# Own orders of a pair of steps for 0 to 6 products, both value bursts in its middle, and row maxima taken 22 steps ahead

## The chip, the cores and the metric

The kernel runs on one core of one Trainium2 chip. The metric is device time in microseconds (us) of one launch; lower is better. Three runs of the kernel before gave 1702.52, 1699.56 and 1701.65 us, so the median is 1701.65 us.

## The reference

```python
def _A_ref(x, wqkv, wo):                     # x (1, 2048, 512), H = 32 heads of Dh = 16
    qkv = (x @ wqkv).reshape(B, S, 3, H, Dh) ...
    scores = jnp.einsum("bhqd,bhkd->bhqk", q, k) * Dh ** -0.5
    p = softmax(scores, axis=-1)
    o = jnp.einsum("bhqk,bhkd->bhqd", p, v)
    return o.reshape(B, S, D) @ wo
def _B_ref(x, w1, b1, w2, b2):               # w1 (2048, 1792), w2 (1792, 2048)
    h = _layernorm(x)
    u = _gelu(jnp.einsum("bsd,sf->bdf", h, w1) + b1)
    return (jnp.einsum("bdf,fs->bds", u, w2) + b2).transpose
xn = _layernorm(x)
return x + _A_ref(xn, wqkv, wo) * _silu(_B_ref(xn, w1, b1, w2, b2))
```

Everything is float32, without a mask: full softmax attention over 2048 tokens with 32 narrow heads, and beside it a two-layer network that mixes tokens.

## The kernel before, in words

Large products are made in three parts from operands split into an upper and a lower half (`three`). The attention is walked in **steps**: one step is one block of 128 keys, for one span of 1024 queries and one pair of heads. There are 512 steps of scores (`NT`) and 512 steps of maxima (`NU`). Softmax needs each query's maximum first, so every score is computed twice:

- `max_of` (L390, L394) makes a 128x512 piece of scores with queries on the partitions, in one of three PSUM banks `mx`; VectorE (DVE) reduces it to one maximum a query.
- `max_rows` (L400 on) is called once in 16 steps. It reduces the collected maxima with a minus sign (L409), turns them by four 32x32 transposes (L406), splits them on GpSimd (POOL; L417, L79), and writes them by four DMAs as two extra rows of the query tile `big` (L83). It returns its work as three pieces, which the loop calls one at a time through `piece()`.
- `score` (L767, L772) makes the transposed piece with keys on the partitions and 50 rows of contraction, the maxima among them, in one of three PSUM banks `sc`. ScalarE (ACT) takes the exponential into a tile `prob`.
- `values` (L783) multiplies the four `prob` tiles of a step with the value block: eight matmuls of 128x32, four side by side. This is called a **burst** here. All 16 key blocks of a span accumulate in the one bank `av`; `put_away` (L522) then copies it out on ACT.

The maxima run `LEAD` = 20 steps ahead of the scores. The token mixer, and after it the output projection, are cut into single **products** (L921 in the main loop, L896 before and after it), which a generator hands out and `take` fetches. A **block** of products accumulates in the one bank `dn`: 48 products for each of the first 14 blocks, then 42 for each of 16, then 9 each for the first 11 blocks of the output projection. At a block's end ACT and POOL work on the result (`gelu`, `silu`, L506 and L507, or `part`), and `take` stops.

The main loop goes over s = 0, 2, 4, ...; two steps make a **pair**. A pair holds 8 maxima, 8 scores, 2 bursts, and n products. All engine queues are strictly in the order in which this loop emits. A product is split into two matmuls on rows 0-63 and 64-127 of the array (`halves`), the maxima and scores of head 0 lie on the lower half and of head 1 on the upper, and the two halves work at the same time. Two strings in `ORDERS`, one for each half, say what is emitted place by place: `D` a product's half, `m` a maximum, `s` a score. One place of the two strings is called a **slot** here. The number behind the strings is the slot ahead of which the first burst stands:

```python
6: ("DDDDDDsmsmsmsm", "msmsmsmsDDDDDD", 7),
```

The second burst stands at the end of the pair. `wanted` spreads the mixer's products up to step 442; what comes out is 6 products in most pairs, what is left (2 for the usual blocks) in the pair that ends a block, and 4 in the pair that begins one. For 5 products the order for 6 is used, with an empty place.

Ahead of the main loop, for s under `LEAD`, maxima alone are made, in groups of three pieces for each head with 11 whole products behind each group (`EARLY`). After step 512 a tail makes the last scores and bursts, with up to 12 whole products behind a burst.

Of the kernel before, what the change touches and what calls it, by code (L numbers as in the profile page):

```python
# [21 lines left out]
def tile_attention_token_mixer(ctx, tc, x, wqkv, wo, w1, b1, w2, b2, out):  # L22
# [7 lines left out]
    NB = S // P  # L30
# [3 lines left out]
    QH = S // 1024  # L34
    SPP = QH * NB
    NT = NP * SPP
    LEAD = 20
    N_BEFORE = 3
    scale = DH ** -0.5

# [113 lines left out]
    with (  # L154
# [214 lines left out]
    def after(n, f):  # L369

        later.append(f if n == 1 else lambda: after(n - 1, f))

    def run_later():
        now, later[:] = list(later), []
        for f in now:
            f()

# [18 lines left out]
    def max_rows(u):  # L396

        p, r = divmod(u // 2, NB)
        span = r // 8
        neg = negs[u // 16 % 2]  # L400
        f = sm.tile([32, P], F32, name="f", bufs=1)


        def turned(*blocks):
            for c in blocks:
                nc.vector.transpose(f[:, 32 * c : 32 * c + 32], neg[32 * c : 32 * c + 32, :])  # L406

        def one():
            nc.vector.tensor_reduce(  # L409
                neg[:, :16].rearrange("p (a b) -> p a b", a=2), mxp.pop(u // 16), axis=AX.X, op=OP.max, negate=True,  # L410
            )
            turned(0)

        def three_():
            turned(3)
            m = sm.tile([16, 2, P], F32R, name="m", bufs=1)
            nc.gpsimd.tensor_copy(m[:, 0, :], f[:16, :])  # L417
            sub(nc.gpsimd, m[:, 1, :], f[:16, :], m[:, 0, :])
            for a in range(2):
                for t in range(2):  # L420
                    row = 64 * a + 48 + t
                    move(
                        qs[p][row : row + 1, span * 1024 : (span + 1) * 1024],
                        m[8 * a : 8 * a + 8, t, :], nc.gpsimd,
                    )

        return one, lambda: turned(1, 2), three_

# [90 lines left out]
    def put_away(p, span, av):  # L519

        ev = el.tile([P, 512], F32, name="ev")
        nc.scalar.copy(ev, av)  # L522
        if p == NP - 1:
            own(span, ev)
            return
        g, i = divmod(p, 4)
        if i == 0:
            dens[span] = sm.tile([P, 64], F32, name="d")
        rows = ev.rearrange("(j r) q -> r j q", r=32)
        for a in range(2):  # L530
# [243 lines left out]
    def values(t):  # L774
        p, r = divmod(t, SPP)
        span, kb = divmod(r, NB)
        if kb == 0:
            state["av"] = ps_av.tile([P, 512], F32, name="av")
        av = state["av"]
        for a in range(2):  # L780
            for c in range(2):
                j = 2 * a + c
                nc.tensor.matmul(  # L783
                    av[32 * j : 32 * j + 32, :],
                    vps[p][:, kb, 16 * a : 16 * a + 32], prob.pop((t, a, c)),
                    start=kb == 0, stop=kb == NB - 1,
                )
        if kb == NB - 1:
            later.append(lambda: put_away(p, span, av))

    def rest():

# [65 lines left out]
    done = 0  # L858
    n_fill = NF * 3 * NB + NB * 3 * NF
    total = NT + LEAD  # L860
    T_MIX = NU - 70
    FIRST = 12
    EARLY = 11
    begun = []

    ended = [False]

    def take(n, each):
# [21 lines left out]
    def whole(x, then):  # L890
# [9 lines left out]


    ORDERS = {
        0: ("smsmsmsm", "msmsmsms", 3),
        2: ("smsmDDsmsm", "msmsmsmsDD", 3),
        4: ("sDDDDmsmsmsm", "msmsmsmDDDDs", 6),
        6: ("DDDDDDsmsmsmsm", "msmsmsmsDDDDDD", 7),
    }

    def halves(lead, n):

# [14 lines left out]
        take(n, each)  # L925
        return *parts, then

    def wanted(s):

        share = min(1.0, (s + 1 - LEAD) / (T_MIX - LEAD))  # L930
        if not begun:
            begun.append(done)
        start = begun[0]
        return start + share * (n_fill - start) + (6 if done == n_fill else 0) if share < 1 else done + 6

    def items(s, a):

# [16 lines left out]
    def piece():  # L954
        if pieces:
            pieces.pop(0)()
            return True
        return False

    lead = 0  # L960
    for s in range(0, total + 1, 2):
        t = s - LEAD
        now[0] = s
        run_later()
        if done >= n_fill // 2 + 3 * NF:
            divisions()
        if s >= NU - 12 and unkept:
            load_second()
        heads = [items(s, a) for a in range(2)]
        if s < NU and t >= 0:  # L970
            steady[0] = True
            late = ended[0]
            n = max(0, min(6, round((wanted(s + 1) - done) / 2) * 2))
            one, two, then = halves(lead, min(n, 4) if late else n)
            made = [dict(D=part, m=heads[a][0], s=heads[a][1]) for part, a in ((one, lead), (two, 1 - lead))]
            first, second, middle = ORDERS[(len(one) + 1) // 2 * 2]
            if one:
                lead = 1 - lead
            for i, kinds in enumerate(zip(first, second)):
                if i == middle:  # L980
                    now[0] = s + 1
                    piece()
                    if 0 <= t - 2 < NT:
                        values(t - 2)
                    run_later()
                for of, kind in zip(made, kinds):
                    if of[kind]:
                        of[kind].pop(0)()
                if "D" in kinds and not two:
                    for f in then:  # L990
                        f()
                    then = []
            for f in then:
                f()
        elif s < NU:

            for i in range(4):
                first_maxima.append((s + i // 2, i % 2))
                if len(first_maxima) == 3 or i == 3 and (s % 16 == 14 or s + 2 == LEAD):
                    for u, half in first_maxima:  # L1000
                        max_of(u, half, 0)
                        max_of(u, half, 1, ps_sc, "sc")
                    first_maxima.clear()
                    take(EARLY, whole)
                if i == 1:
                    now[0] = s + 1
                    run_later()
        else:
            made = [heads[a][1] for a in range(2)]
            n = len(made[0])  # L1010
            for i in range(n):
                made[1][i]()
                made[0][i]()
                if i == n - 2:
                    if not piece() and asides:
                        asides.pop(0)()
                    values(t - 2)
                    take(3 * ND, whole)
                    now[0] = s + 1
                    run_later()  # L1020
            if 0 <= t - 1 < NT and (t - 1, 0, 0) in prob:
                if n:
                    if not piece() and asides and s < total - 2:
                        asides.pop(0)()
                    values(t - 1)
                    if s == total - 2:
                        load_gates(NB // 2, NB - 2)
                    take(3 * ND, whole)
            if s == total - 6:
                split_last_w()  # L1030
        if s < NU and s % 16 == 14:
            pieces.extend(max_rows(s + 1))
        while piece() and t < 0:
            pass
        for v in (t - 2, t - 1):
            if 0 <= v < NT and (v, 0, 0) in prob:
# [16 lines left out]
    left = []  # L1053
    for k in range(4):
        chunk(ps, of, slice(k * P, (k + 1) * P))
    while open_ or later:
        run_later()
        take(3, lambda x, f: left.append(f) if f else whole(x, f))
    for f in left:
# [42 lines left out]
```

## Time and profile before

| | |
|---|---|
| median of three runs | 1701.65 us |
| profiled execution | 1699.51 us |
| its span, first to last instruction | 1697.7 us |
| mean granted TensorE clock | 0.997 |
| TensorE matmul (PE) / weight load (PEld) | 1662.0 us / 842.7 us |
| VectorE / ScalarE / GpSimd | 1425.0 / 1188.0 / 566.5 us |

Between the profiled execution and its span lie 1.8 us. The matmuls of the two halves overlap, and so do those of a burst, so the busy time of PE says only that some matmul was under way. In rows of the timeline the columns are start, duration, engine, line, operation, output and input, count, and in brackets the idle time ahead with what ended it.

### The profile page before, as it was taken

What the parts mean: (1) busy time and instruction counts of PE and PEld (TensorE: products, weight loads), DVE (VectorE), ACT (ScalarE), POOL (GpSimd) and SP (SyncE); (2) the same over time, 40 slices, a digit from 0 to 9 for tenths busy, and PEclk for the clock granted to TensorE, in tenths of its full rate; (3) what the DMA queues carried; (4) which work ended last, traced back from release to release, by engine and by line L of the source; (5) the groups of instructions that cost most, each with busy time, mean ns of one, the idle gap of its engine ahead of it and who ended that gap; (6) DMA issues with size and microseconds to landing.
All of it is one profiled execution on the core that took longest, in us unless ns stands there. A gap on an engine that the chain in (4) does not pass through costs nothing.

```text
span 1697.7 us, 30716 instructions
## 1 busy us (share of the span) xinstructions
PE 1662.0 (98%) x11693; PEld 842.7 (50%) x11693; DVE 1425.0 (84%) x2476; ACT 1188.0 (70%) x2292; POOL 566.5 (33%) x671
## 2 busy tenths in 40 slices
PE   7999999999999999989999999999999999999997
PEld 6887644444444444444444444444444444444443
DVE  6655998888888888878888888888889988889845
ACT  3332277777777777767777777777777777787764
POOL 3223843234342344323322322222222222372411
PEclk9999999999999999999999999999999999999999
DMA  6568612415150513553241514141412223273345
GB/s 211 186 238 190 131 35 57 73 45 85 45 80 26 92 46 54 148 128 91 60 82 53 92 35 76 35 83 35 66 48 43 52 50 68 82 147 102 116 139 197
DMA packets 151311, 153.72 MB, mean 91 GB/s; under 512 B 51500, under 2 KB 109868, under 8 KB 148092
## 3 DMA queue, kind: packets, MB, share of 16 engines
q1 hardware_dynamic: 146748, 151.02, 37.1%
q8 instruction: 92, 1.51, 0.4%
q0 software_dynamic: 4416, 0.75, 0.3%
q14 instruction: 55, 0.45, 0.1%
HBM read 100.81 MB, written 49.79 MB: 89 GB/s over the span
## 4 chain that ended last, share of the span: by engine, by line
PE 90%; DVE 5%; DMA 2%; ACT 1%; POOL 1%; issue 1%; SPq 0%; DVEq 0%; POOLq 0%
PE av L783 27%; PE dn L921 26%; PE mx L390 13%; PE sc L767 11%; DVE mxp L394 4%; PE dn L896 3%; PE mx L303 2%; PE sc L303 2%; PE av L896 1%; ACT prob L772 1%; PE dn L303 1%; PE av L303 1%; DMA big<-m 1%; PE mx L767 0%; PE sc L86 0%
## 5 line engine op out<-in xcount | busy, mean ns | idle before, releaser
L394 DVE TENSOR_REDUCE mxp<-mx 128x1 f32<-128x512 f32 x2008 | 1248.1, 681 | 164.8 <-PE mx L390 85.1
L772 ACT ACTIVATE prob<-sc 128x512 f32<-128x512 f32 x2008 | 1041.8, 604 | 330.4 <-PE sc L767 269.2
L390 PE MATMUL mx<-big 48*128 48x512 f32 x2008 | 827.7, 428 | 2.6 <-DVE mxp L394 0.8
L767 PE MATMUL sc<-big 50*128 50x512 f32 x2008 | 769.2, 427 | 8.2 <-DMA big<-m 6.7
L921 PE MATMUL dn<-hu,wh 64*128 64x512 f32 x1570 | 573.2, 405 | 0.0
L783 PE MATMUL av<-prob,vp 128*32 128x512 f32 x4096 | 546.0, 605 | 0.0
L390 PEld LDWEIGHTS mx<-big 48*128 48x128 f32 x2008 | 364.0, 186 | 222.3 <-DVE mxp L394 208.1
L767 PEld LDWEIGHTS sc<-big 50*128 50x128 f32 x2008 | 354.5, 185 | 195.2 <-ACT prob L772 170.6
L921 PEld LDWEIGHTS dn<-hu,wh 64*128 64x128 f32 x1570 | 288.7, 185 | 171.8 <-issue 144.9
L921 PE MATMUL dn<-hu,wl 64*128 64x512 f32 x786 | 315.7, 402 | 0.9 <-POOL wl L79 0.9
L148 POOL CAST wh<-raw 128x512 fp32r<-128x512 f32 x108 | 62.9, 583 | 319.3 <-PE dn L921 315.1
L79 POOL TENSOR_TENSOR wl<-raw,wh 128x512 fp32r<-128x512 f32 x124 | 150.4, 1216 | 38.0 <-ACT wh L150 22.7
L783 PEld LDWEIGHTS av<-prob,vp 128*32 128x32 f32 x4096 | 80.9, 108 | 154.9 <-issue 146.5
L921 PEld LDWEIGHTS dn<-hu,wl 64*128 64x128 f32 x786 | 145.6, 185 | 9.4 <-POOL wl L79 1.3
L417 POOL CAST m<-f 16x128 fp32r<-16x128 f32 x32 | 9.0, 280 | 281.2 <-DVE f L406 281.2
L474 POOL TENSOR_TENSOR sq<-u 128x512 f32<-128x512 f32 x14 | 14.6, 1040 | 200.3 <-ACT u L473 200.3
L83 POOL DMA_DIRECT2D big<-m x128 | 66.2, 524 | 0.0
L921 PE MATMUL dn<-wh,hu 64*128 64x512 f32 x132 | 45.7, 399 | 0.0
L79 POOL TENSOR_TENSOR hu<-hx,hu 128x512 fp32r<-128x512 f32 x16 | 20.4, 1290 | 57.1 <-ACT hu L246 57.1
L772 ACT ACTIVATE prob<-mx 128x512 f32<-128x512 f32 x40 | 24.7, 617 | 17.6 <-PE sc L767 9.5
L303 PE MATMUL mx<-xt,big 128*128 128x512 f32 x144 | 35.3, 393 | 0.0
L303 PE MATMUL sc<-xt,big 128*128 128x512 f32 x144 | 34.6, 389 | 0.0
(200 smaller groups left out, 1088.7 us busy)
## 6 DMA issues: line engine op xcount, KB each, us to landing
raw<-in_B_w_dram SPq DMA_DIRECT2D x104, 256.0 KB
big<-k_d SPq DMA_DIRECT2D x96, 128.0 KB
big<-q_d SPq DMA_DIRECT2D x96, 128.0 KB
q_d<-sg SPq DMA_DIRECT2D x16, 512.0 KB
k_d<-sg SPq DMA_DIRECT2D x16, 512.0 KB
num_d<-ev SPq DMA_DIRECT2D x30, 256.0 KB
u_d<-uo SPq DMA_DIRECT2D x14, 512.0 KB
hu<-u_d SPq DMA_DIRECT2D x14, 512.0 KB
```

What stands on the lines that cost most here:

```text
L79: eng.tensor_tensor(out=o, in0=a, in1=b.bitcast(F32), op=OP.subtract)
L83: queue.dma_start(dst.bitcast(F32), src.bitcast(F32))
L148: nc.gpsimd.tensor_copy(whs[n][:, :m, :], raws[n][:, :m, :])
L303: nc.tensor.matmul(ps, w[part][:, kd, m], xt[kd][:, z, :], start=w is wh and z == 0 and kd == 0, stop=w is wl and kd == ND - 1,)
L390: nc.tensor.matmul(ps, q[o : o + 48, r * P : (r + 1) * P], k[o : o + 48, c * 512 : (c + 1) * 512], start=True, stop=True,)
L394: nc.vector.tensor_reduce(mxp[u // 16][:, a, r % 8, c : c + 1], ps, axis=AX.X, op=OP.max)
L474: nc.gpsimd.tensor_tensor(out=sq, in0=u, in1=u, op=OP.mult)
L767: nc.tensor.matmul(ps, ks[p][o : o + 50, kb * P : (kb + 1) * P], qs[p][o : o + 50, at : at + 512], start=True, stop=True,)
L772: nc.scalar.activation(e, ps, AF.Exp, scale=scale)
L783: nc.tensor.matmul(av[32 * j : 32 * j + 32, :], vps[p][:, kb, 16 * a : 16 * a + 32], prob.pop((t, a, c)), start=kb == 0, stop=kb == NB - 1,)
L896: nc.tensor.matmul(ps, w(slice(0, P)), m(slice(0, P)), start=first, stop=last)
L921: made.append(lambda r=r, start=first and a == lead, stop=last and a != lead: nc.tensor.matmul(ps, w(r), m(r), start=start, stop=stop,))
```

## The change

- **Orders.** `ORDERS` has an entry for 0, 2, 3, 4, 5 and 6 products, and each names two slots: both bursts now stand inside the pair. `ENDS` has orders for a pair of 4 or 5 products that ends a block, `BEGINS` two for a pair of 4 that begins one; `order` chooses.
- **Counts.** `count` replaces `wanted`: a block is cut into 6 products a pair, except 4 in the pair that begins it and 4 and 4 in its last two (4 and 5 for blocks of nine).
- **Putting away.** The copy of a finished span goes to `soon`: two slots behind the second burst, or at the next call of `run_later`.
- **Maxima.** `LEAD` is 22. `max_rows` returns four pieces (the reduction, one transpose, two transposes, the last with the split and the DMAs), and one is called ahead of each of the two bursts; none at the pair's end any more.
- **Loading.** `load_second` starts at step 502 instead of 500.

```diff
-    LEAD = 20
+    LEAD = 22
...
-        return one, lambda: turned(1, 2), three_
+        return largest, lambda: turned(0), lambda: turned(1, 2), last
...
-            later.append(lambda: put_away(p, span, av))
+            soon.append(lambda: put_away(p, span, av))
...
     ORDERS = {
-        0: ("smsmsmsm", "msmsmsms", 3),
-        2: ("smsmDDsmsm", "msmsmsmsDD", 3),
-        4: ("sDDDDmsmsmsm", "msmsmsmDDDDs", 6),
-        6: ("DDDDDDsmsmsmsm", "msmsmsmsDDDDDD", 7),
+        0: ("ssmmmssm", "msmssmms", 3, 8),
+        2: ("mmsmDDsssm", "ssmsmsmmDD", 3, 10),
+        3: ("DDDsssmmsmm", "ssmmmmssDDD", 4, 7),
+        4: ("DDDDsmsmmssm", "smsmmsmsDDDD", 4, 7),
+        5: ("DDDDDmmsmsmss", "mmsmsssmDDDDD", 5, 8),
+        6: ("DDDDDDsmmsmsms", "msmssmmsDDDDDD", 4, 8),
     }
+    ENDS = {4: ("DDDDmsmssmms", "smsmsmDDDDsm", 4, 10), 5: ("DDDDDssssmmmm", "smsmsmmDDDDDs", 6, 12)}
+    BEGINS = [
+        {4: ("smDDDDsmsmms", "msmsmsmsDDDD", 1, 7)},
+        {4: ("DDDDmssmsmsm", "mmsssmsmDDDD", 5, 8)},
+    ]
+    def order(n, t, late, ends):
+        of = BEGINS[done > n_fill or t % NB == 2] if late else ENDS if ends else ORDERS
+        n = min(x for x in ORDERS if x >= n)
+        return of.get(n, ORDERS[n])
...
+    sizes = [3 * NB] * NF + [3 * NF] * NB + [3 * (ND - 1)] * PARTS
+    def count(late):
+        left = -done
+        for n in sizes:
+            left += n
+            if left > 0:
+                break
+        return 4 if late or left in (7, 8) else 5 if left == 9 else max(0, min(6, left))
...
-            for i, kinds in enumerate(zip(first, second)):
-                if i == middle:
-                    now[0] = s + 1
+            for i, kinds in enumerate((*zip(first, second), "")):
+                if i in places:
                     piece()
-                    if 0 <= t - 2 < NT:
-                        values(t - 2)
-                    run_later()
+                    v = t - 2 + places.index(i)
+                    if v >= 0:
+                        values(v)
+                    if v == t - 2:
+                        now[0] = s + 1
+                        run_later()
+                if i == places[1] + 2:
+                    while soon:
+                        soon.pop()()
...
-        while piece() and t < 0:
+        while t < 0 and piece():
```

More of the change, by code (lines that the diff above doesn't have):

```diff
@@ L371, in after @@
         later.append(f if n == 1 else lambda: after(n - 1, f))
+    soon = []
     def run_later():
-        now, later[:] = list(later), []
+        now, later[:] = soon + later, []
+        soon.clear()
         for f in now:
@@ L406, in turned, with largest @@
                 nc.vector.transpose(f[:, 32 * c : 32 * c + 32], neg[32 * c : 32 * c + 32, :])
-        def one():
+        def largest():
             nc.vector.tensor_reduce(
@@ L411, in one, with last @@
             )
-            turned(0)
-        def three_():
+        def last():
             turned(3)
@@ L860, in tile_attention_token_mixer @@
     total = NT + LEAD
-    T_MIX = NU - 70
     FIRST = 12
     EARLY = 11
-    begun = []
     ended = [False]
@@ L926, in halves @@
         return *parts, then
[L928 to L934, printed above, removed]
+    sizes = [3 * NB] * NF + [3 * NF] * NB + [3 * (ND - 1)] * PARTS
[6 more added lines that the diff above has]
+        return 4 if late or left in (7, 8) else 5 if left == 9 else max(0, min(6, left))
     def items(s, a):
@@ L966, in tile_attention_token_mixer @@
             divisions()
-        if s >= NU - 12 and unkept:
+        if s >= NU - SPP + LEAD and unkept:
             load_second()
@@ L972, in tile_attention_token_mixer @@
             late = ended[0]
-            n = max(0, min(6, round((wanted(s + 1) - done) / 2) * 2))
-            one, two, then = halves(lead, min(n, 4) if late else n)
+            one, two, then = halves(lead, count(late))
             made = [dict(D=part, m=heads[a][0], s=heads[a][1]) for part, a in ((one, lead), (two, 1 - lead))]
-            first, second, middle = ORDERS[(len(one) + 1) // 2 * 2]
+            first, second, *places = order(len(one), t, late, bool(then))
             if one:
                 lead = 1 - lead
-            for i, kinds in enumerate(zip(first, second)):
-                if i == middle:
-                    now[0] = s + 1
+            for i, kinds in enumerate((*zip(first, second), "")):
+                if i in places:
                     piece()
-                    if 0 <= t - 2 < NT:
-                        values(t - 2)
-                    run_later()
+                    v = t - 2 + places.index(i)
[7 more added lines that the diff above has]
+                        soon.pop()()
                 for of, kind in zip(made, kinds):
@@ L1055, in tile_attention_token_mixer @@
         chunk(ps, of, slice(k * P, (k + 1) * P))
-    while open_ or later:
+    while open_ or later or soon:
         run_later()
```

## The prediction

> **What bounds the kernel now.** The page first, for the engines; then the waits, the chain, and the timeline of one block's end.
>
> ```profile
> span 1697.7 us, 30716 instructions
> ...
> PE 1662.0 (98%) x11693; PEld 842.7 (50%) x11693; DVE 1425.0 (84%) x2476; ACT 1188.0 (70%) x2292; POOL 566.5 (33%) x671
> ...
> L772 ACT ACTIVATE prob<-sc 128x512 f32<-128x512 f32 x2008 | 1041.8, 604 | 330.4 <-PE sc L767 269.2
> ```
>
> PE's 98% would leave 36 us in the whole span. The Trainium skill, "Perfetto Trace Analysis", section "Identifying the Most-Contended Engine", calls matmul busy time a poor measure of headroom. The trace agrees: the waits show stalls of weight loads that the matmul row covers, 379 us of them on two rows, though each also contains time that earlier matmuls still fill.
>
> ```profile
> PEld mx L390 <- DVE mxp L394: 208.1, 305, 1.1
> ...
> PEld sc L767 <- ACT prob L772: 170.6, 489, 1.1
> ...
> PE sc L767 <- DMA big<-m: 6.7, 3, 5.0
> ```
>
> So PE waits for a free bank: a maximum for DVE's reduction three maxima back, a score for ACT's exponential three scores back. The chain of waits shows where it repeats (start, duration):
>
> ```profile
> 191.59 2.73 PE dn L896 x11
> ...
> 195.21 2.72 PE dn L896 x11
> ...
> 199.12 2.71 PE dn L896 x11
> ...
> 202.50 2.73 PE dn L896 x11
> ```
>
> ```profile
> 341.60 1.57 DMA big<-m
> ...
> 639.67 2.57 DVE mxp L394 x4
> 690.86 2.57 DVE mxp L394 x4
> ...
> 752.71 5.37 DMA big<-m
> ...
> 1346.71 2.56 DVE mxp L394 x4
> 1392.18 2.56 DVE mxp L394 x4
> ```
>
> DVE ends a wait once a block, and gives the period: 51.19 us for a block of 48 (9 pairs), 45.47 for one of 42 (8 pairs). Inside, PE's timeline around one block's end:
>
> ```profile
> 929.57 1.07 PE L783 MATMUL av<-prob,vp 128*32 128x512 f32 x8
> ...
> 932.44 1.07 PE L783 MATMUL av<-prob,vp 128*32 128x512 f32 x8
> ...
> 935.32 1.07 PE L783 MATMUL av<-prob,vp 128*32 128x512 f32 x8
> 936.32 0.50 PE L767 MATMUL sc<-big 50*128 50x512 f32 x1
> ...
> 936.66 0.40 PE L767 MATMUL sc<-big 50*128 50x512 f32 x1
> ...
> 937.22 1.06 PE L783 MATMUL av<-prob,vp 128*32 128x512 f32 x8
> ...
> 940.59 1.07 PE L783 MATMUL av<-prob,vp 128*32 128x512 f32 x8
> ...
> 946.28 1.07 PE L783 MATMUL av<-prob,vp 128*32 128x512 f32 x8
> ```
>
> From burst to burst, 7 slots take 2.87 and 2.88 us, the 3 slots after 935.32 take 1.90. The line through both: 1.17 us for a burst with its two changes of array shape, and 0.243 a slot. A pair with two bursts should take 2.34 + 0.243 x slots: 14 slots 5.74 (pairs of 6 take 5.75, they lose nothing); 12 slots 5.26; 10 slots 4.77. But the pair of 2 takes 5.27 (935.32 to 940.59) and the pair of 4 behind it 5.69 (to 946.28). Together 0.93 us is lost a block. Why, DVE and ACT show:
>
> ```profile
> 930.74 0.22 DVE L409 TENSOR_REDUCE neg<-mxp 128x16 f32<-128x64 f32 x1
> 931.06 0.20 DVE L406 STREAM_TRANSPOSE f<-neg 32x32 f32<-32x32 f32 x1
> ...
> 933.66 0.41 DVE L406 STREAM_TRANSPOSE f<-neg 32x32 f32<-32x32 f32 x2
> ...
> 936.49 0.20 DVE L406 STREAM_TRANSPOSE f<-neg 32x32 f32<-32x32 f32 x1
> 936.89 4.95 DVE L394 TENSOR_REDUCE mxp<-mx 128x1 f32<-128x512 f32 x8 [0.20 <-PE sc L767]
> ```
>
> ```profile
> 941.19 0.73 ACT L506 ACTIVATE ev<-dn,b2h 128x512 f32<-128x512 f32 x1
> 941.95 0.63 ACT L507 ACTIVATE t<-ev 128x512 f32<-128x512 f32 x1
> 942.48 2.04 ACT L772 ACTIVATE prob<-sc 128x512 f32<-128x512 f32 x4
> ```
>
> DVE needs 4.95 / 8 = 0.62 a maximum, 4.95 a pair: more than the 4.77 of the pair of 2. ACT needs 2.04 / 4 = 0.51 an exponential, 4.1 a pair; the gate's 1.36 us stand ahead of the next pair's scores.
>
> **The change part by part.**
>
> *Counts.* A block of 42 had 6 x 14 + 10 + 12 = 106 slots and now has 5 x 14 + 3 x 12 = 106: PE's own work does not move. Without loss a block takes 106 x 0.243 + 8 x 2.34 = 44.5 us, one of 48 50.3. So at most 45.47 - 44.5 = 0.95 and 51.19 - 50.3 = 0.9 can be won in a block; there are 15 and 10 regular ones, 23 us. Below nothing it can go too, if the new orders stall PE more.
>
> *Orders at a block's end.* I step through the three pairs of 4 (second last, end, begin): a maximum goes out when DVE has ended the third one before it. The stretches from burst to burst hold 3, 9, 6, 3, 6, 9 slots with 3, 5, 4, 3, 4, 5 maxima; PE gives 1.90, 3.36, 2.63, 1.90, 2.63, 3.36, DVE asks 1.86, 3.10, 2.48, 1.86, 2.48, 3.10. Each fits by itself, since DVE works off two maxima during a burst. In blocks of 42 all of `max_rows` falls here (0.22 + 0.20 + 0.41 + 0.20 = 1.03 us): 14.88 + 1.03 = 15.9 of DVE against 15.8 of PE. Stepped, PE waits 0.11 before the last maximum of the second stretch, 0.23 in the third, 0.2 in the last two: 0.53; without `max_rows` 0.17. The same stepping gives 0.40 for the old pair of 2, where 5.27 - 4.77 = 0.50 is measured, so I add 0.1: 0.65 for blocks of 42, and 0.4 for those of 48, whose ends meet `max_rows` only at times. The gate's two ACT operations now come after slot 9 of the ending pair; the burst of 1.17 right behind, and another three slots on, give ACT time to catch up: stepped, 0.1 for one score, which falls together with DVE's wait. `dn` is next written after slot 1 and a burst, when ACT has long read it. Win: 15 x (0.95 - 0.65) + 10 x (0.9 - 0.4) = **9.5 us**.
>
> *Orders of pairs of 6.* The stretches become 4 and 10 slots instead of 7 and 7, with 3 and 5 maxima: 2.14 and 3.60 us against 1.86 and 3.10 of DVE. The three maxima in slots 5 to 7 find three free banks; stepped, no wait for DVE nor ACT. Sum unchanged at 5.74: **0**. The cover is the slack of 0.8 us a pair on DVE; without it, the second rival.
>
> *Blocks of nine.* Measured, pair by pair:
>
> ```profile
> 1591.57 1.07 PE L783 MATMUL av<-prob,vp 128*32 128x512 f32 x8
> ...
> 1597.06 1.06 PE L783 MATMUL av<-prob,vp 128*32 128x512 f32 x8
> ...
> 1602.84 1.06 PE L783 MATMUL av<-prob,vp 128*32 128x512 f32 x8
> ```
>
> 5.49 for 4 products and 5.78 for 5, as the order for 6 has an empty place. The new orders have 12 and 13 slots: 5.26 + 5.50 = 10.76 against 11.27. Stepped, they do not stall; I leave 0.1: 11 x 0.4 = **4.4 us**.
>
> *Maxima earlier.* The fourth piece comes ahead of the second burst, one pair after the old third one's pair; the rows are needed one pair later as well. Of its own pair there now lie 6 slots and a burst behind it, 2.6 us more room for POOL's split, its four DMA issues and their landing. The waits above count 6.7 us of PE for these rows, 5.0 of it once, for the landing of 5.37; and PE was slow behind that (a window each, with its length, busy times, clock, DMA share and GB/s):
>
> ```profile
> 752.00:758.00 6.00, 1.26 (x11) 0.29 (x3) 1.54 (x3) 0.40 (x1) 3.09 (x5) 0.75 0.99 134
> 758.00:761.00 3.00, 2.78 (x11) 1.94 (x11) 1.38 (x2) 1.47 (x3) 0.00 (x0) 0.50 1.09 123
> ```
>
> The granted clock (third last column) falls to 0.50 for 3 us, which costs 1.5 more. The Trainium skill, "TensorE: Matmul & The Clock Gate", Part 1, says an idle window halves the clock; this row agrees. Together 8.2 us; a small rest may stay, as the slow landing needs all the room: **7 us** won, bounds 0 and 8.2. The transposes beside new work on DVE are counted above; On POOL the split and its DMA issues move past a pair's other work, weight splits above all, which nobody waits for here; on SP `load_second` alone moves, a pair later.
>
> *Lead.* Ahead of the loop stands one more group of three maxima pieces, and a group of two becomes one of three: from the rows at 191.59, four groups of (3.62 + 3.91) / 2 instead of two and one of 3.38, +4.1 us. One pair of 6 with bursts goes, -5.75, and 5 products that the group did, -1.2. In the tail stands one more pair, with no products ready for it: ACT's 8 x 0.51 = 4.1 us, at most a whole tail pair with 6 products, 5.1 us:
>
> ```profile
> 1658.77 1.07 PE L783 MATMUL av<-prob,vp 128*32 128x512 f32 x8
> ...
> 1663.88 1.07 PE L783 MATMUL av<-prob,vp 128*32 128x512 f32 x8
> ```
>
> Net **+1.3 us**, bounds 0 and 4. Putting away earlier: the copy has its whole way of eight slots before the next span's first burst; nothing.
>
> *Sum.* 9.5 + 4.4 + 7 - 1.3 = 19.6 us off 1699.5: 1679.9 for a run like the profiled one, and 2.1 more for the median of the runs shown: **1682 us**.
>
> **The rivals.**
>
> *Nothing is lost any more (chance 0.13).* Stepping overstates the waits, as DVE's reductions start while PE still streams. All of 23 + 5.6 (11 x 0.51) + 8.2 - 1.3 = 35.5 us goes: 1666.
>
> *DVE becomes the bound at block ends (0.10).* Three pairs of 12 slots in a row leave DVE 0.3 us each, and `max_rows` needs 1.03. If waits there stay at 0.9 a block, the win is 4.4 + 7 - 1.3 = 10 us: 1692. The Trainium skill, "TensorEngine Tiling (Array Packing)", section "PSUM Bottleneck", says that tiling speeds up PE but not the emptying of PSUM, which is this case. For it: DVE's 14.88 of 15.8; against it: the old pair of 2 asked 4.95 of 4.77.
>
> *Slower: the bursts four slots apart stall the pairs of 6 (0.08).* The new counts make 141 of them, and they lose nothing now. If ACT, with its other copies, comes too late for a score behind the second burst, each pays up to one exponential, 0.51; at 0.2 us it is 28 us, and the kernel ends at 1710. It decides from 20 / 141 = 0.14 us a pair on. Against it: ACT asks 4.1 of 5.74.
>
> *It doesn't do what it says (0.04).* The DMA waits stay, as other DMAs hold them up, and block ends too; with 4.4 of the nines and 4 lost in the tail, 1701.
>
> **How the numbers follow.** The forecast has 0.65, with its own range 1674 to 1691. Reaching to the first two rivals, the range is 1665 to 1696. About 0.2%, 3.4 us, can be told from no change. Faster: 0.65 + 0.13 + 0.10 = 0.88; same 0.04; slower 0.08.
>
> **What would show it.** Bursts in pairs of 6 at 2.14 and 3.60 us; block periods of 45.2 (42) and 50.7 (48) in the chain; 10.8 for two pairs of a block of nine; no granted clock of 0.5 near 750; PEld's wait for DVE below 208. Wrong it is if pairs of 6 take over 5.8, if the periods stay, or if the tail grows by more than 5 us.

## The result, and the profile after

| | before | after |
|---|---|---|
| median, four runs each | 1701.64 us | 1687.47 us |
| range of the runs | 1699.56 to 1702.52 | 1686.77 to 1689.24 |
| profiled execution / its span | 1699.51 / 1697.7 us | 1686.77 / 1684.6 us |

The ratio is 0.9919, interval [0.9907, 0.9932]: 14.2 us faster, where 19.6 were forecast. 1687.5 lies inside the range of 1665 to 1696.

The page of the changed kernel, engines and the exponential's group (its columns: busy time and mean ns, then idle time ahead and what ended most of it):

```profile
span 1684.6 us, 30617 instructions
...
PE 1653.2 (98%) x11682; PEld 874.7 (52%) x11682; DVE 1419.8 (84%) x2478; ACT 1191.0 (71%) x2293; POOL 565.9 (34%) x668
...
L774 ACT ACTIVATE prob<-sc 128x512 f32<-128x512 f32 x2004 | 1048.4, 604 | 316.5 <-PE sc L769 209.5
```

PE stays at 98%: its busy time falls by 8.8 us in a span that is 13.1 us shorter, so that row says little. The waits of the changed kernel (total, times, longest):

```profile
PEld mx L393 <- DVE mxp L397: 258.7, 356, 0.9
...
PEld sc L769 <- ACT prob L774: 85.8, 162, 1.4
...
PE sc L769 <- DMA big<-m: 2.4, 2, 1.4
```

The wait of weight loads for ACT halved (170.6 before), that for DVE rose (208.1 before), and the kernel became faster. So these two rows can't be read as lost time: most of their time is covered by matmuls already in the array. What is lost shows only from burst to burst. Here is a block's end in the changed kernel: the second last pair, the ending pair and the beginning pair (the timeline of PE and its weight loads: the bursts, and one score's weight load, with its idle time ahead in brackets):

```profile
919.50 1.06 PE L785 MATMUL av<-prob,vp 128*32 128x512 f32 x8
...
921.38 1.06 PE L785 MATMUL av<-prob,vp 128*32 128x512 f32 x8
...
924.76 1.06 PE L785 MATMUL av<-prob,vp 128*32 128x512 f32 x8
...
926.97 0.18 PEld L769 LDWEIGHTS sc<-big 50*128 50x128 f32 x1 [0.45 <-ACT prob L774]
...
927.63 1.06 PE L785 MATMUL av<-prob,vp 128*32 128x512 f32 x8
...
929.51 1.06 PE L785 MATMUL av<-prob,vp 128*32 128x512 f32 x8
...
932.22 1.07 PE L785 MATMUL av<-prob,vp 128*32 128x512 f32 x8
```

By the line 1.17 + 0.243 x slots, 3 slots take 1.90, 6 take 2.63 and 9 take 3.36. Measured: 1.88 for 3 slots (919.50 to 921.38), 3.38 for 9, 2.87 for 6 (to 927.63), 1.88 for 3, 2.71 for 6 (to 932.22). The stretch that loses most is that of 6 slots to 927.63, by 0.24, and in it stands the weight load that waits for ACT. The 9 slots behind the last row, to 935.75, lose another 0.17.

**The whole difference in the terms of the prediction.** I took every stretch from burst to burst of the main loop, subtracted the line, and summed what is left (us lost; a stretch belongs to the step of the pair in which it ends; the block that changes the size from 48 to 42 lies in steps 206 to 226):

| steps | before | after | of it waits for rows of maxima, before / after |
|---|---|---|---|
| to 206 (blocks of 48) | 11.2 | 10.9 | 1.6 / 4.9 |
| 206 to 226 | 9.3 | 3.1 | 7.0 / 0 |
| 226 to 466 (15 blocks of 42) | 16.0 | 7.7 | 0 / 0 |
| 466 to 512 (blocks of nine) | 6.1 | 9.7 | 0 / 0 |
| sum | 42.6 | 31.4 | 8.6 / 4.9 |

The losses fell by 11.2. The rest is schedule: the loop has 30 slots fewer (3237 to 3207; 11 of them the empty places in blocks of nine, the others went to the lead) and two bursts fewer, 9.6 us by the line; against that the first burst comes 2.0 later (212.77 to 214.73), the additional tail pair takes 4.1 (its bursts at 1595.24 and 1599.37), and the rest of the tail is 1.5 longer (83.7 to 85.2). 11.2 + 9.6 - 2.0 - 4.1 - 1.5 = 13.2, and the span fell by 13.1. In the next table, block ends are the first three rows without the waits for rows of maxima (27.9 before, 16.8 after); lead and tail are 2.0 + 4.1 + 1.5 less the two bursts and the 19 slots that left the loop (2.3 + 4.6). A third late row of the kernel before (0.6 us of waiting at step 370, about 0.4 lost) is left among the block ends; counted as a row, it would make them -10.7 and the rows -4.1.

| term | forecast | measured |
|---|---|---|
| block ends | -9.5 | -11.1 |
| pairs of 6 | 0 | 0 (4 slots 2.13 to 2.14; 10 slots 3.52 to 3.59 in 101 of 140 stretches, 3.82 or 3.83 in 22 with a put-away copy); what they lose and gain stands in the block ends |
| blocks of nine | -4.4 | -2.7 by slots, +3.6 by waits: +0.9 |
| rows of maxima | -7 | -3.7 |
| lead and tail | +1.3 | +0.7 |
| sum | -19.6 | -13.2 |

Two terms were far off. First the nines, in two places. One is the first block of nine, around step 470, by the chain of waits of the changed kernel (start, duration):

```profile
1469.57 1.74 POOL big L83 x4
...
1471.66 2.53 POOL hu L79 x2
1474.19 1.24 POOL u L587
1475.43 1.24 POOL sq L587
1476.66 0.55 POOL wh L148
...
1477.30 1.28 POOL wl L79
...
1478.62 0.50 PE dn L935
```

POOL works here almost without a pause: the DMAs of a row of maxima, the splits of one division (`hu`), the multiplications of the next (`u`, `sq`), and only then the weights (`wh`, `wl`) of the product for which PE stands. The pairs at 468 and 470 lose 4.0 us together, 2.5 before. The other place is further on:

```profile
1499.59 1.08 ACT prob L774 x2
1500.66 1.02 ACT hu L599 x2
1501.68 0.51 ACT prob L774
...
1502.24 0.50 PE sc L769
```

ACT also casts the result of a division into `hu`, two casts of 1.02 us together. The ending order for 5 products puts four scores in a row ("ssss"). Where the casts fall between these scores' exponentials, PE waits some 1.0 us for a bank (pairs at steps 478 and 502). Two pairs without such a wait take 10.94, within 0.14 of the forecast 10.8, where they took 11.23 before.

Then the rows of maxima. The chain before the one long wait:

```profile
697.50 1.89 DVE mxp L397 x3
...
700.50 1.15 POOL big L83 x3
...
702.06 5.93 DMA big<-m
```

and the windows around it (length, PE, PEld, DVE, ACT, POOL, granted clock, DMA share, GB/s):

```profile
700.00:704.00 4.00, 4.00 (x34) 1.98 (x34) 3.29 (x7) 3.14 (x7) 3.88 (x7) 1.00 0.84 222
704.00:708.00 4.00, 2.74 (x23) 1.46 (x15) 3.65 (x6) 2.21 (x5) 0.56 (x1) 1.00 0.94 318
708.00:712.00 4.00, 3.88 (x21) 1.82 (x21) 0.90 (x2) 1.68 (x3) 0.00 (x0) 0.68 0.52 189
```

The four small DMAs of the rows (4 KB each) were under way for 5.93 us while 318 GB/s of data moved, with four loads `hu<-u_d` of 512 KB issued between 698 and 710. PE had a gap of 1.4 us, and then ran at a mean clock of 0.68 for 4 us: in slices of 1 us the clock is 0.50 from 710 to 712 and 1.00 again from 713. Together about 3.5 us. The other late row, at 433.28, landed in the usual 1.58 us, but POOL came to it late. It cost 1.4; the clock stayed at 1.00 there. DVE had its last transpose done at 427.9, and POOL took up the row 3.0 us later. POOL's timeline ahead of it has two operations of `gelu` (L476, L478) before the rows' cast and DMAs:

```profile
427.88 1.04 POOL L476 TENSOR_TENSOR sq<-u 128x512 f32<-128x512 f32 x1 [20.93 <-ACT u L475]
...
429.71 1.30 POOL L478 TENSOR_TENSOR sq<-sq,u 128x512 f32<-128x512 f32 x1
430.94 0.28 POOL L419 CAST m<-f 16x128 fp32r<-16x128 f32 x1
```

### The profile page after: what moved, and what is told of

Read it like the earlier page. It is cut to its first block, busy times and chain, and to the rows that moved or that the text cites. A ratio compares the mean times of both kernels' runs of the same rounds, so it can differ in the third digit from the quotient of the medians.

```text
span 1684.6 us, 30617 instructions
## 1 busy us (share of the span) xinstructions
PE 1653.2 (98%) x11682; PEld 874.7 (52%) x11682; DVE 1419.8 (84%) x2478; ACT 1191.0 (71%) x2293; POOL 565.9 (34%) x668
## 4 chain that ended last, share of the span: by engine, by line
PE 92%; DMA 2%; DVE 2%; POOL 2%; ACT 1%; issue 0%; SPq 0%; DVEq 0%; POOLq 0%; ACTq 0%
PE av L785 29%; PE dn L935 23%; PE mx L393 16%; PE sc L769 12%; PE dn L895 2%; PE mx L303 2%; PE sc L303 2%; DVE mxp L397 1%; PE dn L303 1%; PE av L303 1%; DMA raw<-in_B_w_dram 1%; PE mx L769 1%; DMA big<-m 0%; DMA big<-k_d 0%; POOL wl L79 0%
## 5 line engine op out<-in xcount | busy, mean ns | idle before, releaser
L769 PE MATMUL sc<-big 50*128 50x512 f32 x2004 | 761.2, 419 | 4.7 <-DMA big<-m 2.4
L393 PE MATMUL mx<-big 48*128 48x512 f32 x2004 | 742.2, 419 | 0.4
L935 PE MATMUL dn<-hu,wh 64*128 64x512 f32 x1556 | 533.4, 403 | 0.0
L393 PEld LDWEIGHTS mx<-big 48*128 48x128 f32 x2004 | 359.0, 186 | 281.3 <-DVE mxp L397 258.7
L769 PEld LDWEIGHTS sc<-big 50*128 50x128 f32 x2004 | 359.6, 185 | 106.1 <-ACT prob L774 85.8
L148 POOL CAST wh<-raw 128x512 fp32r<-128x512 f32 (+1 forms) x107 | 62.4, 583 | 321.0 <-PE dn L935 190.0
L476 POOL TENSOR_TENSOR sq<-u 128x512 f32<-128x512 f32 x14 | 14.6, 1042 | 184.6 <-ACT u L475 184.6
```

The costliest lines, as they stand in the source:

```text
L148: nc.gpsimd.tensor_copy(whs[n][:, :m, :], raws[n][:, :m, :])
L393: nc.tensor.matmul(ps, q[o : o + 48, r * P : (r + 1) * P], k[o : o + 48, c * 512 : (c + 1) * 512], start=True, stop=True,)
L476: nc.gpsimd.tensor_tensor(out=sq, in0=u, in1=u, op=OP.mult)
L769: nc.tensor.matmul(ps, ks[p][o : o + 50, kb * P : (kb + 1) * P], qs[p][o : o + 50, at : at + 512], start=True, stop=True,)
L935: made.append(lambda r=r, start=first and a == lead, stop=last and a != lead: nc.tensor.matmul(ps, w(r), m(r), start=start, stop=stop,))
```

## The experiments

Each run has beside it runs of the kernel before on the same chip; there its medians were 1702.01 (e1 to e4), 1702.14 (e5 to e8) and 1701.52 (e9 to e12). "Changed kernel with" means that only the edit shown was made to it.

### The lead alone, in the kernel before

```diff
-    LEAD = 20
+    LEAD = 22
...
-            if s >= NU - 12 and unkept:
+            if s >= NU - SPP + LEAD and unkept:
```

> The kernel before with LEAD 22 alone: old orders, old counts, three pieces of the maxima at their old places. My theory: the lead costs about 1 us net (one more group ahead of the loop and one more pair in the tail, against one pair of 6 and 5 products fewer), and the query rows are needed a pair later, so PE no longer waits 5.0 us for them once and the clock does not fall: 1693 to 1698 us. Rival (the late rows come from other DMAs, not from too little room): the wait stays and the lead only costs, 1702 to 1705 us.

Measured: 1701.25 us, 0.9997 [0.9987, 1.0006]. No change, though not one wait of a score for a row is left in the waits. The forecast missed; the gain was given back. With a lead of 22 the pieces of `max_rows` move by a pair against the products, and the gate's pair of 2 now has them in it. The timeline of this kernel there:

```profile
1152.05 1.06 PE L783 MATMUL av<-prob,vp 128*32 128x512 f32 x8
...
1153.64 0.41 DVE L406 STREAM_TRANSPOSE f<-neg 32x32 f32<-32x32 f32 x2
1153.99 3.03 DVE L394 TENSOR_REDUCE mxp<-mx 128x1 f32<-128x512 f32 x5
...
1154.68 0.50 PE L390 MATMUL mx<-big 48*128 48x512 f32 x1 [0.42 <-DVE mxp L394]
...
1155.71 1.07 PE L783 MATMUL av<-prob,vp 128*32 128x512 f32 x8
```

The 7 slots from 1152.05 to 1155.71 take 3.66 where the line gives 2.87: 0.79 lost instead of 0.50 in the same place before. Over all blocks this stretch loses 19.3 instead of 13.0 us. The blocks of nine lose 9.9 instead of 6.1, all of the difference in the pairs at 466 and 468, the first block of nine again. So the waits for rows, 8.6 us of loss, went, and 6.3 and 3.8 came: the loop loses 44.6 us instead of 42.6. Of the 3.8, some 1.7 are 3.4 us at a clock of 0.50, behind a gap of 1.7 us at 1486.8.

### The changed kernel with the old lead

```diff
-    LEAD = 22
+    LEAD = 20
```

> The changed kernel with LEAD back at 20, four pieces as changed. My theory: the fourth piece now has only the 6 slots and the burst behind it, 2.6 us, before the first score that needs its rows, while split, issues and landing take 0.7 + 2.1 + 1.6 = 4.4 us; PE waits about 1.8 us in each of some 30 spans, and longer where POOL is late: 1735 us or more. Rival (the room behind the last piece does not matter, the lead of 22 is only a cost): 1685 to 1688 us.

Measured: 1830.8 us, 1.0762 [1.0746, 1.0778]. The row of the waits, and a window with one of them:

```profile
PE sc L769 <- DMA big<-m: 80.5, 30, 5.7
```

```profile
708.00:716.00 8.00, 5.22 (x24) 2.22 (x21) 2.26 (x5) 2.26 (x4) 3.69 (x6) 0.66 0.02 4
```

Nearly every row is late now: with four pieces, one a burst, two more steps of lead are needed. 80.5 us are waited in 30 places, yet the kernel is 143 us longer than with 22. The window shows one reason for the difference: the granted clock is 0.66 over 8 us. The mean clock of the whole run is 0.965 (0.997 before). Over a span of 1828 us that is 58 us of clock, an estimate from above, as PE stands still in part of it; with the 80.5 it makes 139 of the 143. The direction was as the theory said; the size was more than its lower bound.

### No own orders at a block's end and begin

```diff
-    ENDS = {4: ("DDDDmsmssmms", "smsmsmDDDDsm", 4, 10), ...}
-    BEGINS = [{4: ("smDDDDsmsmms", ...)}, {4: ("DDDDmssmsmsm", ...)}]
+    ENDS = {}
+    BEGINS = [{}, {}]
```

> The changed kernel without ENDS and BEGINS: pairs at a block's end and begin take the common order for their count. My theory: the gate's two ACT operations come behind the last slot again, the next pair's scores wait for them, and products of the next block stand in its first slots, while ACT still reads dn: some 0.4 us more in each of 25 block ends and 11 blocks of nine, 1698 to 1705 us. Rival (the even counts alone bring the gain at block ends): within 3 us of the changed kernel, 1687 to 1690 us.

Measured: 1758.37 us, 1.0327 [1.0277, 1.0377], 71 us above the changed kernel. That is far over the range. The waits name the cause:

```profile
PE dn L932 <- ACT ev L508: 22.5, 16, 1.4
...
PE dn L932 <- ACT t L705: 15.8, 10, 1.9
...
PE dn L932 <- ACT u L475: 14.6, 10, 1.9
```

The order for 4 begins with `D`. After a block's end the first product of the next block stands in PE's queue ahead of everything else and waits until ACT has read `dn`, 52.9 us in 36 places, up to 1.9 each, with nothing beside it that could run. The waits of the changed kernel have no row of `dn` for ACT. The mean clock fell to 0.983 as well, 25 us over the span by the same estimate. The theory had this wait in it, but took it and the late scores together for 0.4 us a block, where one wait is 1.5 on average.

### The changed kernel with the old begin alone

```diff
-    BEGINS = [{4: ("smDDDDsmsmms", ...)}, {4: ("DDDDmssmsmsm", ...)}]
+    BEGINS = [{}, {}]
```

> The changed kernel with its own orders for a pair that ends a block, but without those for a pair that begins one: that pair takes the common order for 4, with products in slots 0 to 3. Without both, PE stood 53 us for ACT's reading of the bank dn, 36 times. My theory: the beginning order is what keeps PE out of that wait, by one slot and a burst ahead of the first product (in blocks of nine by the end order's early last product); with the end order alone ACT reads dn some 0.6 us earlier, so half of the 71 us comes back: 1710 to 1735 us. Rival (the end order alone is enough, since it starts the gate before its second burst): within 5 us of the changed kernel, 1687 to 1693 us.

Measured: 1699.27 us, 0.9983 [0.9974, 0.9992], 11.8 above the changed kernel, between what the theory and the rival had given. The wait for `dn` is gone but for 1.2 us once. So the end order clears it: its last product stands in slot 9 (the first is slot 0), with a burst and two slots behind it, where the order for 4 has one in its last slot. What is lost stands in the timeline:

```profile
887.70 1.07 PE L785 MATMUL av<-prob,vp 128*32 128x512 f32 x8
888.31 0.71 ACT L508 ACTIVATE ev<-dn,b2h 128x512 f32<-128x512 f32 x1
...
889.59 2.04 ACT L774 ACTIVATE prob<-sc 128x512 f32<-128x512 f32 x4
890.22 0.50 PE L769 MATMUL sc<-big 50*128 50x512 f32 x1
890.89 1.06 PE L785 MATMUL av<-prob,vp 128*32 128x512 f32 x8
```

The gate's operations on ACT hold up the exponentials, and 6 slots take 3.19 instead of 2.63. This stretch loses 11.5 us in the 26 large blocks and 0.27 in each of the 11 blocks of nine; the whole loop loses 44.0 instead of 31.4. So of the 71 us the begin orders carry 12, and the end orders, alone or with them, the rest.

### The old order of pairs of 6

```diff
-        6: ("DDDDDDsmmsmsms", "msmssmmsDDDDDD", 4, 8),
+        6: ("DDDDDDsmsmsmsm", "msmsmsmsDDDDDD", 7, 14),
```

> The changed kernel with the old order for 6 products, its bursts at slot 7 and at the pair's end. My theory: a pair of 6 has 0.8 us to spare on DVE in either order and loses nothing in both, so it stays within 2 us: 1685 to 1690 us. Rival (the two bursts close together are what brings the gain): 5 us slower or more, 1692 us upwards; if they cost, faster than 1685.

Measured: 1694.24 us, 0.9962 [0.9951, 0.9974], 7 above the changed kernel. A pair of 6 among others of its kind loses nothing either way. But behind a beginning pair, whose bursts stand ahead of slots 1 and 7 of 12 in these 25 blocks, the old order leaves a stretch of 12 slots without a burst:

```profile
890.06 1.06 PE L785 MATMUL av<-prob,vp 128*32 128x512 f32 x8
...
894.55 1.06 PE L785 MATMUL av<-prob,vp 128*32 128x512 f32 x8
```

4.49 instead of the 4.09 of the line. The sum is 25 times 0.41, where the changed kernel loses 25 times 0.18 in its own stretch there: 5.8 of the 7. So the bursts in the middle bring something, but only next to block ends; I had put that at nothing.

### Counts, lead and pieces, with all old orders

`ORDERS` has the four old pairs of strings for 0, 2, 4 and 6 products with the second burst at the end, there is no `ENDS` or `BEGINS`; the counts, the lead of 22 and the four pieces stay.

> The changed kernel with all old orders: bursts at the old slots (the second at the pair's end), no own ends and begins; the new counts, the lead of 22 and the four pieces stay. My theory: the gate still falls between two pairs of 4, each of them keeps the 0.2 to 0.4 us that it lost before, and the query rows come in time: 1691 to 1697 us. Rival (the even counts 4, 4, 4 instead of 6, 2, 4 are the gain at block ends, whatever the order): 1685 to 1689 us.

Measured: 1697.35 us, 0.9974 [0.9965, 0.9984]. That is 0.4 above the range of the theory. Blocks of 42 take 45.51 us, as before (45.47): 15 of them lose 16.2 us, before 16.0. So the new counts by themselves win nothing at a block's end, and the 0.5 of a block come from the orders. As to what it does win: the pairs of 206 to 226 lose 2.3 instead of 9.3, as the long wait for a row is gone; 4.1 of it are lost again in blocks of nine (10.2 instead of 6.1, at steps 468 and 470). These 2.9 us are not the whole 4.8 of the medians, and the two profiled runs differ by only 1.6, so the rest is not accounted for.

### Two pieces a burst, for rows that are sooner ready

With the old lead (first) and with the new one (second), a second call in the loop:

```diff
                 if i in places:
                     piece()
+                    piece()
```

> The changed kernel with LEAD 20 and two pieces of the maxima ahead of each burst, so that all four are called in one pair and the rows have the same room (8.4 us) as with LEAD 22 and one piece. My theory: the waits for the rows, which cost 144 us with LEAD 20 and one piece at a time, are gone; the lead's group and tail pair are saved, up to 0.4 us of DVE in a lump costs at most 0.2 us a span: 1682 to 1690 us. Rival (it is the lead by itself that matters, for instance for the banks): far slower, above 1720 us.

> The changed kernel, LEAD 22, with two pieces of the maxima ahead of each burst: the rows get one pair more room (14 us instead of 8.4) at the same phase of blocks and spans. My theory: the two waits for late rows that are left (about 1.4 us in one pair, 3.5 us with the slow landing in another) go, and the lumped DVE work costs up to 0.1 us in 31 spans: 1682 to 1687 us. Rival (lumped DVE work stalls the pairs of 4 at block ends): slower than the changed kernel, 1689 us or more.

Measured: 1708.88 us, 1.0038 [1.0026, 1.0051], and 1694.84 us, 0.9961 [0.9948, 0.9973]. Both slower than the changed kernel; both forecasts missed, and in the second the rival held. With lead 22 no score waits for a row any more, so 4.9 us are won; but the blocks of 42 take 45.47 instead of 44.97. The timeline ahead of the ending pair's first burst:

```profile
922.83 1.07 PE L785 MATMUL av<-prob,vp 128*32 128x512 f32 x8
...
924.43 0.63 DVE L409 STREAM_TRANSPOSE f<-neg 32x32 f32<-32x32 f32 x3
924.99 3.03 DVE L397 TENSOR_REDUCE mxp<-mx 128x1 f32<-128x512 f32 x5
...
926.71 1.07 PE L785 MATMUL av<-prob,vp 128*32 128x512 f32 x8
```

Three transposes in one place hold DVE for 0.63, and the 9 slots take 3.88 instead of the 3.36 of the line. The 15 blocks of 42 lose 14.6 us instead of 7.7, those of 48 another 4.8, which is more than the rows gave. With lead 20 the rows cost 3.3 us of waits only, but all blocks of 42 now take the other of the two begin orders, lose 0.6 in its first stretch, and take 45.62. Another 7 us go in the blocks of nine (16.7 instead of 9.7), most of it in the pair at step 480. Both show the rule of DVE at a block's end from the other side: a row must be ready early, but its work on DVE must not come in one piece.

### Division sooner, and its casts apart

```diff
-        after(8 if g < ND - 1 else 4, two)
+        after(8 if g < ND - 1 else 2, two)
```

> The changed kernel with the reciprocal of the last group of heads one pair earlier, so that products are ready for the first pair of the tail, which has none in the changed kernel. My theory: that pair of 4.1 us, set by ACT alone, takes in products that lengthen later pairs: 2 to 4 us faster than the changed kernel, 1683 to 1686 us. Rival (the tail is set by ACT or by its end, not by products): 1687 us, no change.

Measured: 1687.8 us, 0.9916 [0.9902, 0.9929], no change against 1687.47. From burst 489 to the end it takes 83.1 instead of 85.2, but the tail pair ahead of it is 3.0 longer (7.1 instead of 4.1); the rival held. The second kernel has this edit and in `parts` one cast and its split now, the other cast and split half a pair later, with the division begun six products sooner:

```diff
-            for c in range(2):
-                o = oc[g, 2 * span + c] = hu.tile([P, 2, 512], F32R, name="hu")
-                nc.scalar.copy(o[rows, 0, :], num[c][rows, :])
-                sub(eng(), o[rows, 1, :], num[c][rows, :], o[rows, 0, :])
-            divided.add((g, span))
+            half(0)
+            later.append(lambda: (half(1), divided.add((g, span))))
...
-        needed = min(n_fill, n_fill - 3 * NF + 6 * m + 6) if m else 0
+        needed = min(n_fill, n_fill - 3 * NF + 6 * m) if m else 0
```

> As the one before, and the two casts that a division hands to ACT stand half a pair apart instead of back to back, and may begin six products earlier. My theory: back to back they take 1.02 us of ACT where the order for 5 products has four scores in a row, and cost a wait of 1.0 to 2.5 us in three pairs of the blocks of nine; apart they cost less: another 2 to 4 us, 1680 to 1683 us. Rival (the waits there come from the order itself): no more than the one before.

Measured: 1688.85 us, 0.9923 [0.9909, 0.9936]. The forecast missed. The waits that the casts made did shrink (step 478 from 1.03 to 0.50, step 502 from 1.01 to nothing), so the casts are their cause. But the pair at 470 loses 5.8 there instead of 2.5, by another chain:

```profile
1470.75 8.39 DMA big<-m
```

The DMAs of the row of maxima were under way for 8.39 us. The 16 DMA engines were 0.93 busy from 1474 to 1480, and among the DMAs issued there are loads for the next division (`uo<-rec_d`, 512 KB, and `sq<-num_d`, 256 KB). In the changed kernel the row's DMAs of the same place met a share of 0.05 (1470 to 1474) and landed in 1.6. So it seems that the sooner division put its loads in the way of the row; no run tests that by itself.

### The second half's maxima and scores exchanged in the pair of 6

```diff
-        6: ("DDDDDDsmmsmsms", "msmssmmsDDDDDD", 4, 8),
+        6: ("DDDDDDsmmsmsms", "smsmsmmsDDDDDD", 4, 8),
```

> The changed kernel with the first four places of the second half in the order for 6 products turned round, so that its maxima stand in slots 1 and 3 instead of 0 and 2. Stepping says: behind a beginning pair the fifth maximum of the stretch of nine slots goes out in slot 2, 0.15 us before DVE has freed its bank (measured 0.18 in 24 of 25 blocks); in slot 3 the bank is free. Everywhere else nothing changes. My theory: 25 x 0.18 = 4.4 us faster than the changed kernel, 1682 to 1685 us. Rival (that 0.18 is not a wait for a bank but belongs to the stretch): no change, 1687 us.

> The two edits before this together: if both theories hold they add, 1677 to 1683 us. If DVE is the common limit, the second takes back what the first gives: 1685 us or more.

The second kernel has this and the second `piece()`. Measured: 1693.48 us, 0.9949 [0.9936, 0.9961], and 1697.13 us, 0.9971 [0.9960, 0.9983]. Both forecasts missed. The 0.18 behind a beginning pair goes, as stepped (9 slots take 3.36). But once in eight pairs a span is put away, by a copy on ACT that the stepping had left out:

```profile
851.25 1.06 PE L785 MATMUL av<-prob,vp 128*32 128x512 f32 x8
...
853.51 0.58 ACT L524 COPY ev<-av 128x512 f32<-128x512 f32 x1
...
855.31 1.06 PE L785 MATMUL av<-prob,vp 128*32 128x512 f32 x8
```

4.06 for 10 slots; the same stretch takes 3.82 in the changed kernel, and 3.60 by the line. With smaller losses of the same kind in other pairs of 6 they lose 10.0 us instead of 2.5, more than the 3.9 that the exchange wins behind beginning pairs; 1.1 of the difference is the late row of step 198. The profiled run, the slowest of the five (1696.23), also loses 2.7 more in blocks of nine. No version here beats the changed kernel.

## Why the prediction was right or wrong

**Right in direction and range**, for its main reason. The block ends lose less, by the orders and not by the counts: the counts with the old orders keep the period of 45.5, the changed kernel has 44.97 in blocks of 42 (forecast 45.2) and 50.78 in an ordinary one of 48 (forecast 50.7). *DVE becomes the bound at block ends* was refuted: the loss of a block of 42 went from 1.07 (16.0 / 15) to 0.51 (7.7 / 15), and half of what is left is ACT's. In the step "0.23 in the third" stretch the size came out and the engine was wrong, so that agreement is luck. The stretch of 6 slots in the ending pair loses 0.25 in all 26 blocks, with and without `max_rows`, because a score waits for the exponential three scores back (the weight load at 926.97); I had put that stall on DVE and only where `max_rows` meets it. One sum is slightly off: a block of 48 without loss is 120 x 0.243 + 9 x 2.34 = 50.2, not 50.3, which would have made the forecast of this term 10.2.

**Pairs of 6: right.** 2.14 and 3.60 were forecast, 2.13 to 2.14 and mostly 3.52 to 3.59 measured; *the bursts four slots apart stall the pairs of 6* is refuted. The term 0 was too simple all the same: next to block ends the new order is worth 7 us against the old one (e4), and behind a put-away copy it loses 0.23.

**Blocks of nine: mis-sized, -4.4 forecast, +0.9 measured.** "Stepped, they do not stall" failed. The stepping had ACT's exponentials in it but not its two casts of a division, 1.02 us, which cost 2.0 in two pairs; and it had nothing of POOL, which makes PE wait for weights in the first block of nine: 1.5 us more than before. The slot that the empty place had cost was won in every block, 2.7 in all.

**Maxima earlier: mis-sized, -7 forecast, -3.7 measured.** "2.6 us more room" was right, and the wait of 5.0 with its clock of 0.5 near 750 is gone. But room is only one side: a landing took 5.93 us when other DMAs moved 318 GB/s, and one row was held up by `gelu` on POOL, which the prediction passed over: of POOL's other work "nobody waits", it said, and the late row of 433.28 and the weights at step 470 both waited for just that queue. The kernel before has three late rows in the profiled run, the changed kernel two, in other places. The bounds of 0 to 8.2 held it. The low clock is not gone either: it is 0.50 here too, but for 3.4 us (709.4 to 712.8) where it was 6.8 (755.0 to 761.8), 3.3 of them within the wait itself. That more room would have been enough is shown by the kernel with two pieces a burst and lead 22: no row waits.

**Lead and tail: right** (+1.3 forecast, +0.7 measured; the additional tail pair 4.13 where 4.1 was worked out).

**PEld's wait for DVE** was to fall below 208 and rose to 258.7: as a sign it was badly chosen, because it counts the time that a weight load stands ready behind matmuls that still run.

**What stays open.** That the row of step 198 lands late because of the loads `hu<-u_d` is not tested. The late rows are not an accident of one run: six variants with the same counts, lead and pieces (the old order of 6, all old orders, the sooner division, the casts apart, no own begins, the exchanged pair) have the same two late, at steps 102 and 198. The first landed in 1.57 to 1.59 us in each of them, the second in 4.79 to 6.69. An ending order with its scores further apart, which would take the 0.25 in the ending pair, was not tried: the products of both halves must then be done in fewer slots.

## What to carry to other kernels

When an order is stepped by hand, put everything that an engine does there into it, the rare copies and casts too: the misses in blocks of nine (casts and POOL's chain) and behind the exchanged pair (the put-away copy) were operations left out of the steps, not wrong durations; the wait of the first product on `dn` was in them and priced far too low. Change the phase between two periodic things (here rows of maxima each 16 steps and blocks each 8 pairs) only with a look at where each piece lands: the lead alone took away all row waits and won nothing. And measure loss from marker to marker (bursts, with a line for the work between them), since the waits of weight loads rose while the kernel became faster.

## What the runs showed of the hardware

A short wait can cost more than its length, but need not. Before, a wait of 5.0 us brought 6.8 us at a granted clock of 0.50. After, a gap of 1.4 us was followed by 3.4 us at 0.50, and one of 1.0 us at 434.0 by none. In the kernel without own orders 27 gaps are 1.42 or 1.43 us long, and 13 of them were followed by 3.4 us at 0.50, the others by none. Here is the time behind two of them, which end at 331.1 and 435.4:

```profile
332.00:336.00 4.00, 4.00 (x33) 1.49 (x31) 3.59 (x8) 2.59 (x6) 3.75 (x5) 1.00 0.00 0
...
435.00:439.00 4.00, 3.61 (x16) 1.32 (x16) 1.49 (x3) 1.44 (x3) 3.81 (x6) 0.58 0.03 4
```

With the old lead 30 waits bring the whole run to 0.965, and of the 143 us that it costs the waits are 80.5. The Trainium skill, "TensorE: Matmul & The Clock Gate", Part 1, says that the clock is halved after at least one idle window of about 3.4 us. The traces agree with the half, and with stretches of 3.4 us or twice that; they do not agree that PE must be idle for so long, since gaps of 1.4 us were enough about half of the time.

Small DMAs have no fixed price. The same four DMAs of 4 KB landed in 1.57 and 1.58 us in two places where the 16 DMA engines were 0.03 busy, and in 5.37 and 5.93 us where they were 0.99 and 0.94 busy; once, in a variant, they took 8.39 (0.93 busy). A distance in steps has to be planned for the larger figures.
